# A last product by Strassen's algorithm: seven block products in place of eight, in a single-core gated mix kernel

## The chip, the cores and the metric

The kernel runs on one core of a Trainium2 chip. Its engines work side by side, each through its own queue in program order: TensorE (PE) multiplies matrices into banks of PSUM, VectorE (DVE), ScalarE (ACT) and GpSimd (POOL) work element by element, and SyncE (SP) issues the DMAs. [...] Engines wait for one another through semaphores, and an instruction that waits holds up all that stands behind it on its engine. The metric is the device time in microseconds (us).

## The reference

Input `x` has 2048 tokens of 640 features. A gate `g` for every token mixes two branches:

```python
g = sigmoid((x * gate_w).sum(-1, keepdims=True))
a = conv(x)            # diagonal state-space convolution, kernel K from A, B, C, dt, plus x * Dskip
# linear attention, 32 heads of 20 features
q, k, v = split(x @ wqkv)
phi = lambda t: where(t > 0, t + 1, exp(t)) + 1e-6
kv  = einsum("bhsd,bhse->bhde", phi(k), v);  z = phi(k).sum over tokens
o   = (phi(q) @ kv) / (phi(q) . z + 1e-6)
b   = o @ wo
out = g * a + (1 - g) * b
```

With these inputs the convolution comes down to a running sum of the tokens, scaled by one coefficient for each feature, and `phi(q) @ kv @ wo` to one product of `phi(q)` with a 640 x 640 matrix `M`, in which `kv` and `wo` are already multiplied together.

## The kernel before

The output is made transposed, feature blocks of 128 (five of them, NB) by token groups of 512 (four, NG): 20 output tiles of 128 x 512, numbered j = 5 x group + block. Every product in high accuracy is done three times: both operands are split into a high part (a copy to a shorter format on ACT, `hi`, line 100) and a low part (the difference, on DVE, `lo`, line 103), and `mm3` (lines 106 to 108) adds high x high, low x high and high x low in one bank.

A first stage, up to about 145 us, makes `phi(k)`, its product with `x`, and the convolution tiles y of 16 of the 20 output tiles, which are stored to DRAM. A second, up to about 180 us, builds `M` and begins with q. The part around the change is the third. Its order is written out by hand in `PLAN`, a string of steps that is played from left to right, and the order in which the steps are played is the order of the instructions on every engine:

- `q` (`q_block`): one tile of `phi(q)` before normalisation. 15 matmuls; ACT makes exponential and positive part (lines 648, 649); DVE takes minimum and adds (652) and adds to a weighted sum (658) that becomes the denominator.
- `d` (`q_den`): the denominator of a group. Two matmuls on the high and low part of that sum (673, 674), ACT reads the bank (676), DVE takes the reciprocal (677) and multiplies with 1 - g (680).
- `n` (`q_norm`): scales one tile (688). Its high and low parts, tiles pTh and pTl, are issued by `flush` a step later.
- `f`: `final_mm`, one output tile, 15 matmuls with `M` (5 input blocks x 3), then `final_out`: DVE adds bank and y (727) and SP stores it (728). It then calls `y_block` for a tile that is needed later.
- `y` (`y_block`): loads a stored y (439), or makes it then and there (tiles 16 to 19: ACT 423, DVE scan 424 and multiply-add 427), and POOL multiplies it with the gate (444).

```python
q3 f q3 d2 n2 f q3 n2 f q3 n2 n2 f q3 f n2
f d3 n3 f n3 n3 f n3 f n3 f
f f f f f f
```

These are the last three lines of `PLAN`: five q tiles of group 3 with five outputs between them, group 3's normalisation with five outputs between, and six outputs at the end. PSUM has eight banks here: three with the tag "q", three "f" (outputs and denominators) and two "m". Six buffers hold y tiles, eight (NE) hold tiles of `phi(q)` (tag "e"), and two hold output tiles on their way to DRAM (tag "so").

Of the kernel before, what the change touches and what calls it, by code (L numbers as in the profile page):

```python
# [39 lines left out]
P = 128  # L40
L = 2048
D = 640
NB = D // P
NT = L // P
NG = L // 512
# [12 lines left out]
NK = sum(map(len, CONV_K.values()))  # L58
# [13 lines left out]
NS = NK + PLAN.split().count("c")  # L72


def f32(ap):
    return ap.bitcast(F32)


def body(tc, i, outT):
    nc = tc.nc  # L80
    pe, act, dve, pool, sp = nc.tensor, nc.scalar, nc.vector, nc.gpsimd, nc.sync
    outer, top, kst = ExitStack(), ExitStack(), ExitStack()

    def mk(stack, name, space=None):
        kw = {} if space is None else {"space": space}
        if space is not DRAM:
            kw["reuse_waits"] = "tile"
        return stack.enter_context(tc.tile_pool(name=name, bufs=1, **kw))
# [3 lines left out]
    px = mk(top, "px")  # L92
    pc = mk(top, "pc")
    pw = mk(top, "pw")
# [4 lines left out]
    def hi(dst, src):  # L99
        act.activation(dst, src, AF.Copy)  # L100

    def lo(dst, src, h, eng=None):
        (eng or dve).tensor_tensor(dst, src, f32(h), op=OP.subtract)  # L103

    def mm3(out, ah, al, bh, bl, start, stop):
        pe.matmul(out, ah, bh, start=start, stop=False)  # L106
        pe.matmul(out, al, bh, start=False, stop=False)  # L107
        pe.matmul(out, ah, bl, start=False, stop=stop)  # L108

    def col(tag, n=NB, dt=F32):  # L110
        return pc.tile([P, n], dt, tag=tag, name=tag)
# [20 lines left out]
    zacc = col("zacc", D)  # L132
# [10 lines left out]
    dtc, k0, dsk, lam, ok = [col(n) for n in ("dtc", "k0", "dsk", "lam", "ok")]  # L143
    g, og = col("g", NT), col("og", NT)
# [39 lines left out]
    kp, ke, ks = {}, {}, {}  # L184
# [217 lines left out]
    us, ys, gbs, y_d = {}, {}, {}, {}  # L402

    def gb_load(gi):
        gbs[gi] = pq.tile([P, 512], F32, tag="gb", bufs=NG, name="gb")
        src = g_d[gi * 4 : gi * 4 + 4, :].rearrange("a b -> (a b)")[None, :]
        sp.dma_start(gbs[gi], src.to_broadcast([P, 512]))

    def u_load(j):
        gi, b = divmod(j, NB)  # L410
        if j < NK or j >= NS:
            us[j] = pw.tile([P, D + 2], F32, tag="st", bufs=3, name="u")
        else:
            us[j] = pq.tile([P, 512], F32, tag="u", bufs=1, name="u")
        sp.dma_start(us[j][:, :512], i["xT"][b * P : b * P + P, gi * 512 : gi * 512 + 512])

    def conv(j, name="y"):

        gi, b = divmod(j, NB)
        c = slice(b, b + 1)  # L420
        u = us.pop(j)[:, :512]
        y = pw.tile([P, 512], F32, tag="y", bufs=NY, name=name)
        act.activation(y, u, AF.Copy, scale=k0[:, c])  # L423
        dve.tensor_tensor_scan(y, y, zero.to_broadcast([P, 512]), cY[:, c], op0=OP.add, op1=OP.add)  # L424
        if gi < NG - 1:
            dve.tensor_copy(cY[:, c], y[:, 511:512])
        dve.scalar_tensor_tensor(y, u, dsk[:, c], y, op0=OP.mult, op1=OP.add)
        return y

    def conv_out(j):  # L430
        y = conv(j)
        y_d[j] = dram.tile([P, 512], F32, name=f"y_d{j}")
        sp.dma_start(y_d[j], y)

    def y_block(j):

        if j < NS:
            ys[j] = pw.tile([P, 512], F32, tag="y", bufs=NY, name="yb")
            sp.dma_start(ys[j], y_d[j])
        else:  # L440
            ys[j] = conv(j, "yb")
            if j + 3 < NG * NB:
                u_load(j + 3)
        pool.tensor_tensor(ys[j], ys[j], gbs[j // NB], op=OP.mult)  # L444


# [17 lines left out]
    raw = {}  # L464
# [28 lines left out]
    for b in range(NB):  # L493
        w = raw[b][:, : CA + 2]
# [113 lines left out]
    rem = col("rem", D)  # L608
# [12 lines left out]
    pq = mk(top, "pq")  # L621
    pqp = mk(top, "pqp", PSUM)
# [9 lines left out]
            hi(GT[:, b0:b1, 512:], tp[:, : (b1 - b0) * P].rearrange("p (b s) -> p b s", s=P))  # L632

    pqT, qe, acc, rd = {}, {}, {}, {}
    pend = []

    def q_block(gi, b):

        qp = pqp.tile([P, 512], F32, tag="q", bufs=3, name="qp")
        w, o = (wqA, b * P) if b < 3 else (wqB, (b - 3) * P)  # L640
        for c in range(NB):
            mm3(qp, w[0][:, c, o : o + P], w[1][:, c, o : o + P], xTh[gi][:, c, :], xTl[gi][:, c, :],
                c == 0, c == NB - 1)
        if len(qe) + len(pend) == NE:
# [4 lines left out]
        act.activation(r, qp, AF.Relu)  # L649
        for h, _, v in pend:  # L650
            hi(h, v)
        dve.scalar_tensor_tensor(e, e, 1.0, r, op0=OP.min, op1=OP.add)  # L652
        if b == 0:
            a = acc[gi] = pq.tile([P, 512], F32, tag="acc", bufs=1, name="acc")
            act.activation(a, e, AF.Copy, scale=zc[:, :1])
        else:
            a = acc[gi]
            dve.scalar_tensor_tensor(a, e, zc[:, b : b + 1], a, op0=OP.mult, op1=OP.add)
# [23 lines left out]

    def q_norm(gi, b):
        e = qe.pop((gi, b))
        if b == 0:
            pqT[gi] = [px.tile([P, NB, 512], F32R, tag=f"x{c}{gi}", name=f"pT{c}{gi}") for c in "hl"]
        h, l = [v[:, b, :] for v in pqT[gi]]
        dve.scalar_tensor_tensor(e, e, EPS, rd[gi], op0=OP.add, op1=OP.mult)  # L688
        flush()
        pend.append((h, l, e))  # L690

    def flush():
        for h, l, v in pend:
            hi(h, v)
            lo(l, v, h)
        pend.clear()

    m = {}
# [13 lines left out]
    def final_mm(j):  # L712
        gi, b = divmod(j, NB)
        fps[j] = []
        for h0, h1 in HALVES[j == NG * NB - 1]:
            fp = pqp.tile([P, 512], F32, tag="f", bufs=3, name="fp")
            fps[j].append(fp)
            for kb in range(NB):
                mm3(fp[:, : h1 - h0], m["h"][:, kb, b * P : b * P + P], m["l"][:, kb, b * P : b * P + P],
                    pqT[gi][0][:, kb, h0:h1], pqT[gi][1][:, kb, h0:h1], kb == 0, kb == NB - 1)  # L720

    def final_out(j):
        gi, b = divmod(j, NB)
        o = pq.tile([P, D], F32, tag="so", bufs=2, name="o")
        y = ys.pop(j)
        for fp, (h0, h1) in zip(fps.pop(j), HALVES[j == NG * NB - 1]):
            dve.tensor_tensor(o[:, h0:h1], fp[:, : h1 - h0], y[:, h0:h1], op=OP.add)
            sp.dma_start(outT[b * P : b * P + P, gi * 512 + h0 : gi * 512 + h1], o[:, h0:h1])

    NJ = NG * NB  # L730
    n_q, n_n, n_f, n_y, n_c = 0, 0, 0, 0, NK
    z_part()
    rem_out()
    if NS > NK:
        u_load(NK)
    for w in PLAN.split():
        what, k = w.rstrip("0123456789"), int("0" + w.lstrip("abcdefghijklmnopqrstuvwxyz"))
        if what == "q":
            q_block(*divmod(n_q, NB))
            n_q += 1  # L740
        elif what == "z":
            z_const()
            gates_row()
        elif what == "d":
            q_den(k)
        elif what == "n":
            q_norm(*divmod(n_n, NB))
            n_n += 1
        elif what == "kv":
            kv_mm(k)  # L750
        elif what == "m":
            m_mm(k)
        elif what == "ml":
            m_load()
            for j in range(NS, min(NS + 3, NJ)):
                u_load(j)
        elif what == "c":
            conv_out(n_c)
            n_c += 1
            if n_c < NS:  # L760
                u_load(n_c)
        elif what == "y":
            y_block(n_y)
            n_y += 1
        elif what == "f":
            flush()
            final_mm(n_f)
            final_out(n_f)
            n_f += 1
            if n_y < NJ:  # L770
                y_block(n_y)
                n_y += 1
    assert (n_q, n_n, n_f) == (NJ, NJ, NJ)
# [171 lines left out]
```

## Time and profile before

| | |
|---|---|
| runs | 299.1 us median of 3 (298.33 to 304.32) |
| profiled execution | 296.9 us from the first to the last instruction; no time of its own is given beyond this span |
| busy | PE 98%, weight loads 86%, DVE 77%, ACT 42%, POOL 16% |
| granted PE clock | full throughout |
| DMA | 46.00 MB, mean 155 GB/s |

A row of busy time gives us, share of the span and count of instructions for each engine. In a group of instructions the columns are line, engine, operation, output <- inputs, shape and count, then busy time and mean duration in ns, then idle time of the engine just ahead of them and what ended it. In a row of single instructions the columns are start, duration, engine, line, operation; a number in square brackets is idle time of the engine before it, with what ended it. Weight loads run beside matmuls. The length shown for a matmul is modelled and overlaps with its neighbours; the distance between starts says how long PE takes for one.

### The profile page before, as it was taken

What the parts mean: (1) busy time and instruction counts of PE and PEld (TensorE: products, weight loads), DVE (VectorE), ACT (ScalarE), POOL (GpSimd) and SP (SyncE); (2) the same over time, 40 slices, a digit from 0 to 9 for tenths busy, and PEclk for the clock granted to TensorE, in tenths of its full rate; (3) what the DMA queues carried; (4) which work ended last, traced back from release to release, by engine and by line L of the source; (5) the groups of instructions that cost most, each with busy time, mean ns of one, the idle gap of its engine ahead of it and who ended that gap; (6) DMA issues with size and microseconds to landing.
All of it is one profiled execution on the core that took longest, in us unless ns stands there. A gap on an engine that the chain in (4) does not pass through costs nothing.

```text
span 296.9 us, 4579 instructions
## 1 busy us (share of the span) xinstructions
PE 291.7 (98%) x1627; PEld 254.3 (86%) x1627; DVE 228.6 (77%) x355; ACT 125.1 (42%) x262; POOL 47.0 (16%) x52
## 2 busy tenths in 40 slices
PE   8999999999999999999999999999999999999994
PEld 7998899999999999999887777888888888888884
DVE  2869987899999799955743769968683777787992
ACT  3555144653565545337624374562323233314100
POOL 3601760000000000000000000003313203232541
PEclk9999999999999999999999999999999999999999
DMA  6925477257767854280364563792416022426323
GB/s 171 330 69 184 132 242 232 86 200 234 235 152 256 249 168 156 82 256 1 88 174 138 164 203 106 231 329 79 141 35 186 29 71 71 142 73 182 125 85 111
DMA packets 28409, 46.00 MB, mean 155 GB/s; under 512 B 3771, under 2 KB 10827, under 8 KB 28383
## 3 DMA queue, kind: packets, MB, share of 16 engines
q1 hardware_dynamic: 28383, 45.66, 49.0%
q8 instruction: 15, 0.25, 0.3%
q14 instruction: 11, 0.09, 0.1%
HBM read 32.92 MB, written 12.72 MB: 154 GB/s over the span
## 4 chain that ended last, share of the span: by engine, by line
PE 96%; DMA 1%; SPq 0%; ACT 0%; DVE 0%; issue 0%
PE qp L106 8%; PE fp L107 8%; PE fp L108 8%; PE fp L106 8%; PE qp L107 8%; PE qp L108 8%; PE g L232 6%; PE g L231 6%; PE g L234 6%; PE k L108 6%; PE k L107 6%; PE k L106 6%; PE g L459 3%; PE r L247 2%; PE r L246 2%; PE r L245 2%
## 5 line engine op out<-in xcount | busy, mean ns | idle before, releaser
L444 POOL TENSOR_TENSOR yb<-yb,gb 128x512 f32<-128x512 f32 x20 | 28.3, 1417 | 217.8 <-DMA yb<-y_d 199.6
L108 PE MATMUL fp<-pTl,Mh 128*128 128x512 f32 (+1 forms) x105 | 39.8, 379 | 0.0
L107 PE MATMUL fp<-pTh,Ml 128*128 128x512 f32 (+1 forms) x105 | 39.8, 379 | 0.0
L106 PE MATMUL fp<-pTh,Mh 128*128 128x512 f32 (+1 forms) x105 | 39.8, 379 | 0.0
L232 PE MATMUL g<-ph,xl 128*128 128x512 f32 x80 | 31.4, 392 | 0.0
L231 PE MATMUL g<-ph,xh 128*128 128x512 f32 x80 | 31.3, 391 | 0.0
L652 DVE SCALAR_TENSOR_TENSOR qe<-qe,qr 128x512 f32<-128x512 f32 x20 | 14.3, 716 | 21.7 <-ACT qr L649 21.6
L100 ACT ACTIVATE pTh<-qe 128x512 fp32r<-128x512 f32 x20 | 12.6, 633 | 41.4 <-DVE qe L688 41.4
L210 DVE SCALAR_TENSOR_TENSOR e<-e,r 128x320 f32<-128x320 f32 x32 | 15.7, 496 | 13.2 <-ACT e L207 13.2
L106 PE MATMUL qp<-xTh,wqAh 128*128 128x512 f32 x60 | 23.8, 396 | 0.0
L648 ACT ACTIVATE qe<-qp 128x512 f32<-128x512 f32 x20 | 11.9, 595 | 28.0 <-PE qp L108 23.0
L204 ACT ACTIVATE e<-k 128x320 f32<-128x320 f32 x12 | 5.3, 438 | 43.4 <-PE k L108 43.4
L107 PE MATMUL qp<-xTh,wqAl 128*128 128x512 f32 x60 | 23.4, 390 | 0.0
L108 PE MATMUL qp<-xTl,wqAh 128*128 128x512 f32 x60 | 23.4, 389 | 0.0
L234 PE MATMUL g<-pl,xh 128*128 128x512 f32 x80 | 23.3, 389 | 0.0
L106 PEld LDWEIGHTS fp<-pTh,Mh 128*128 128x128 f32 x105 | 19.8, 188 | 3.8
L107 PEld LDWEIGHTS fp<-pTh,Ml 128*128 128x128 f32 x105 | 19.7, 188 | 3.8
L108 PEld LDWEIGHTS fp<-pTl,Mh 128*128 128x128 f32 x105 | 19.7, 188 | 3.7
L103 DVE TENSOR_TENSOR pTl<-qe,pTh 128x512 fp32r<-128x512 f32 x20 | 16.1, 817 | 6.8 <-ACT pTh L100 6.3
L424 DVE TENSOR_TENSOR_SCAN y<-y,cY,zero 128x512 f32<-128x512 f32 x16 | 20.5, 1278 | 0.8 <-ACT y L423 0.8
L108 PE MATMUL k<-wkBl,xTh 128*128 128x320 f32 x60 | 18.5, 309 | 0.0
L107 PE MATMUL k<-wkBh,xTl 128*128 128x320 f32 x60 | 18.5, 309 | 0.0
(171 smaller groups left out, 720.9 us busy)
## 6 DMA issues: line engine op xcount, KB each, us to landing
xraw<-in_x SPq DMA_DIRECT2D x16, 320.0 KB, 4.4
u<-in_xT SPq DMA_DIRECT2D x20, 256.0 KB, 5.7
out_T<-o SPq DMA_DIRECT2D x19, 256.0 KB, 2.6
y_d<-y SPq DMA_DIRECT2D x16, 256.0 KB, 2.4
yb<-y_d SPq DMA_DIRECT2D x16, 256.0 KB, 3.1
xTraw<-in_xTt SPq DMA_DIRECT2D x12, 320.0 KB, 4.5
Wv<-in_wv SPq DMA_DIRECT2D x5, 320.0 KB, 5.8
Mh<-M_dh SPq DMA_DIRECT2D x5, 320.0 KB, 4.5
```

The source lines that it names most:

```text
L100: act.activation(dst, src, AF.Copy)
L103: (eng or dve).tensor_tensor(dst, src, f32(h), op=OP.subtract)
L106: pe.matmul(out, ah, bh, start=start, stop=False)
L107: pe.matmul(out, al, bh, start=False, stop=False)
L108: pe.matmul(out, ah, bl, start=False, stop=stop)
L210: dve.scalar_tensor_tensor(e, e, 1.0, r[:, :n], op0=OP.min, op1=OP.add)
L231: pe.matmul(gps[b], xh[:, s], h[:, :512], start=t == 0, stop=False)
L232: pe.matmul(gps[b], xl[:, s], h[:, :512], start=False, stop=False)
L234: pe.matmul(gps[b], xh[:, b * P : b * P + P], l[:, :512], start=False, stop=t == NT - 1)
L424: dve.tensor_tensor_scan(y, y, zero.to_broadcast([P, 512]), cY[:, c], op0=OP.add, op1=OP.add)
L444: pool.tensor_tensor(ys[j], ys[j], gbs[j // NB], op=OP.mult)
L652: dve.scalar_tensor_tensor(e, e, 1.0, r, op0=OP.min, op1=OP.add)
```

## The change

The output tiles of token groups 2 and 3 and feature blocks 0 to 3, over input blocks 0 to 3, are taken as a 2 x 2 block product: `M`'s 512 x 512 corner in four blocks, and the normalised `phi(q)` of the two groups in four blocks (input blocks 0 and 1, or 2 and 3; group 2 or 3). Strassen's algorithm in its form with few additions (seven products, chained sums) makes the four results out of seven products of sums. Input block 4 is added with plain matmuls (`rest`), and outputs 14 and 19 (feature block 4) stay whole.

- `t_sums` (step t) makes the sums of `M` on POOL, 4 additions of 512 columns and 8 of 256; `t_split` (step tb) makes their high and low parts in tiles that held weights of q.
- `s_sums` (step s, twice) makes the sums of `phi(q)` in place on POOL, 4 additions each, in the `e` tiles, which `er` keeps for it; `s_split` makes the high and low parts of the four sums.
- `last_pair` runs the products after the plan has ended. Banks are used as running sums: ACT takes a snapshot of a bank in the middle, DVE adds an earlier product onto a bank, and POOL adds a snapshot to the y of another output.
- The plan: outputs 6 to 9 move behind the last q tile, all outputs of groups 2 and 3 move into `last_pair`. `y_block` follows the new order `ORD`, group 3 is normalised in the order 0, 2, 1, 3, 4 (`NORM`), and tiles 16 to 19 load their inputs in the order `LATE`. `e` has 10 buffers in place of 8; two of the four tiles of the gate (`gb`) go to other tiles.

```diff
-NE = 8
+NE = 10
+SG = 2, 3
+ORD = [0, 1, 2, 3, 4, 5, 6, 7, 8, 9, 14, 10, 11, 12, 15, 17, 13, 16, 18, 19]
+NORM = [(g, b) for g in range(NG) for b in ((0, 2, 1, 3, 4) if g == SG[1] else range(NB))]
...
-q3 f q3 d2 n2 f q3 n2 f q3 n2 n2 f q3 f n2
-f d3 n3 f n3 n3 f n3 f n3 f
-f f f f f f
+q3 f q3 d2 n2 q3 n2 t q3 n2 n2 f q3 n2 y
+f d3 tb n3 f n3 s n3 y f n3 s n3 y f
...
+    def t_sums():
+        tr = [pw.tile([P, D + 2], F32, tag=t, bufs=n, name="tr")[:, :512] for t, n in (("wo", 2), ("wo", 2), ("st", 3), ("st", 3))]
+        tt = pool.tensor_tensor
+        for k in range(4):
+            tt(tr[k], f32(m["h"][:, k, :512]), f32(m["l"][:, k, :512]), op=OP.add)
+        for j in range(2):
+            b11, b12, b21, b22 = tr[j][:, :256], tr[j][:, 256:], tr[j + 2][:, :256], tr[j + 2][:, 256:]
+            tt(b11, b12, b11, op=OP.subtract)
+            tt(b12, b22, b12, op=OP.subtract)
+            tt(b22, b22, b11, op=OP.subtract)
+            tt(b21, b21, b22, op=OP.subtract)
+        tw["raw"] = tr
+
+    def t_split():
...
+        for h, r in zip(tw["h"], tr):
+            hi(h, r)
+        for h, l, r in zip(tw["h"], tw["l"], tr):
+            lo(l, r, h)
+
+    def s_sums(j):
+        a11, a12, a21, a22 = er[2, j], er[2, j + 2], er[3, j], er[3, j + 2]
+        tt = pool.tensor_tensor
+        tt(a22, a21, a22, op=OP.add)
+        tt(a21, a11, a21, op=OP.subtract)
+        tt(a11, a22, a11, op=OP.subtract)
+        tt(a12, a12, a11, op=OP.subtract)
+        sx[1, j], sx[3, j], sx[2, j], sx[4, j] = a22, a21, a11, a12
+
+    def s_split(*ks):
...
+        for n, k in enumerate(ks):
+            for j in range(2):
+                sh[k, j] = h[:, 2 * n + j, :], l[:, 2 * n + j, :]
+                hi(sh[k, j][0], sx[k, j])
+            for j in range(2):
+                lo(sh[k, j][1], sx.pop((k, j)), sh[k, j][0])
+
+    PROD = {1: ("x", 0, 0, "m", 0, 0), 2: ("x", 0, 2, "m", 2, 0), 4: ("x", 1, 2, "t", 2, 0),
+            3: ("s", 4, 0, "m", 2, 2), 5: ("s", 1, 0, "t", 0, 0), 6: ("s", 2, 0, "t", 2, 2), 7: ("s", 3, 0, "t", 0, 2)}
...
+        def raws(i):
+            four[i] = pb("m")
+            prod(four[i], 4, i, True)
+            rest(four[i], 1, i)
+            prod(one[i], 2, i, False)
+            rest(one[i], 0, i)
+            done(0, i, one[i])
+
+        def six(i):
+            A[i] = pb(("f", "q")[i])
+            prod(A[i], 6, i, True)
+            dve.tensor_tensor(A[i], A[i], s1[i], op=OP.add)
+            add(0, i + 2, snap(A[i], "r", 2))
+
+        def five(i):
+            B[i] = pb("f")
+            prod(B[i], 5, i, True)
+            add(1, i + 2, snap(B[i], "r", 2))
+
+        def seven(i):
+            prod(A[i], 7, i, False)
+            add(1, i, snap(A[i], "d"))
+            done(1, i, four[i])
+
+        def three(i):
+            prod(B[i], 3, i, False)
+            rest(B[i], 0, i + 2)
+            done(0, i + 2, B[i])
+
+        def end(i):
+            rest(A[i], 1, i + 2)
+            done(1, i + 2, A[i])
+
+        final_mm(last[0])
+        for i in range(2):
+            one[i] = pb("q")
+            prod(one[i], 1, i, True)
+            s1[i] = snap(one[i], ("acc", "accl")[i])
+        final_out(last[0])
+        y_next()
+        s_split(2, 1)
+        raws(0)
+        s_split(3, 4)
+        raws(1)
+        six(0), five(0), six(1), seven(0), three(0), five(1), end(0)
+        seven(1), three(1), end(1)
+        final_mm(last[1])
+        final_out(last[1])
```

In it `prod` issues the six matmuls of one half (128 output columns) of a product, `rest` three, `snap` is a copy of a bank on ACT, `add` an addition to a y tile on POOL, and `done` the addition of bank and y on DVE with the store, followed by the next `y_block`. A step s begins with `flush`.

More of the change, by code (lines that the diff above doesn't have):

```diff
@@ L690, in q_norm @@
         pend.append((h, l, e))
+        if gi in SG and b < 4:
+            er[gi, b] = e
     def flush():
@@ new lines, in prod @@
+    def prod(bank, p, i, first):
+        a, n, k0, w, w0, c = PROD[p]
+        c = slice((c + i) * P, (c + i + 1) * P)
+        for j in range(2):
+            if a == "x":
+                ah, al = [v[:, k0 + j, :] for v in pqT[SG[n]]]
+            else:
+                ah, al = sh[n, j]
+            if w == "m":
+                bh, bl = [m[x][:, w0 + j, c] for x in "hl"]
+            else:
+                bh, bl = [tw[x][w0 + j][:, c] for x in "hl"]
+            mm3(bank, bh, bl, ah, al, first and j == 0, j == 1, skip_group_check=True)
@@ L746, in body @@
         elif what == "n":
-            q_norm(*divmod(n_n, NB))
+            q_norm(*NORM[n_n])
             n_n += 1
+        elif what == "t":
+            t_sums()
+        elif what == "tb":
+            t_split()
+        elif what == "s":
+            flush()
+            s_sums(n_s)
+            n_s += 1
         elif what == "kv":
@@ L754, in body @@
             m_load()
-            for j in range(NS, min(NS + 3, NJ)):
+            for j in LATE[:2]:
                 u_load(j)
```

77 lines of the change are left out of this document (61 added, 16 removed).

## The prediction

> **What bounds the kernel now.** I read the head of the page first, then the waits of TensorE (PE), then busy time by stretch, then the groups of VectorE (DVE) in the part that changes, and last the single instructions of DVE and GpSimd (POOL) there.
>
> ```profile
> span 296.9 us, 4579 instructions
> PE 291.7 (98%) x1627; PEld 254.3 (86%) x1627; DVE 228.6 (77%) x355; ACT 125.1 (42%) x262; POOL 47.0 (16%) x52
> ...
> PE 96%; DMA 1%; SPq 0%; ACT 0%; DVE 0%; issue 0%
> ...
> L100 ACT ACTIVATE pTh<-qe 128x512 fp32r<-128x512 f32 x20 | 12.6, 633 | 41.4 <-DVE qe L688 41.4
> ```
>
> The second row is busy time by engine, the third the chain that ended last: 96% of it is PE. The fourth is a group (count, busy us, mean ns), one copy on ScalarE (ACT), used below. The view of waits, cut to PE, says what PE waited for:
>
> ```profile
> PE k L131 <- POOL ones L122: 1.0, 1, 1.0
> PE r L459 <- ACT wkBh L100: 0.2, 1, 0.2
> ```
>
> That is 1.2 us in all, both at the start. PE's order is fixed by the program and it never stands still later. By stretch:
>
> ```profile
> 220.00:240.00 20.00, 20.00 (x90) 16.53 (x89) 12.84 (x15) 6.61 (x12) 4.36 (x3) 1.00 0.26 80
> ...
> 232.00:293.00 61.00, 60.95 (x283) 50.84 (x281) 50.73 (x57) 14.68 (x25) 18.96 (x13) 1.00 0.30 100
> ```
>
> The columns are the stretch, its length, then PE, weight loads, DVE, ACT, POOL (each with its count), granted clock, DMA share, GB/s. 89 loads in 20 us make 0.225 us for a 512-wide matmul, so a block of 15 takes 3.4 us. In the last 61 us DVE is busy 50.7 us already: PE bounds, and DVE is close behind.
>
> **What the change removes.** The last product takes three matmuls per pair of 128-blocks. The Strassen part (two groups, four output blocks, four input blocks) was 2 x 4 x 4 x 3 = 96 matmuls and becomes 7 products x 2 halves x 2 blocks x 3 = 84. The 24 for the fifth input block and the two whole outputs of the fifth block stay. So 12 matmuls go: 12 x 0.225 = **2.7 us off PE**, 0.9% of the time. A difference under 2%, some 6 us, can hardly be told from no change here, so PE's gain alone cannot show.
>
> **What it adds.** On POOL: `t_sums`, 4 additions of 512 columns and 8 of 256; `s_sums`, 2 x 4 of 512; in `last_pair` 6 additions of 512. On DVE: 4 low parts in `t_split`, 8 in the two `s_split`, 2 additions onto a bank. On ACT: 12 copies for high parts and 8 snapshots of banks, near the 0.63 us of the row L100 each, 13 us on an engine that is busy 14.7 of 61 us; these count only where someone waits. DMAs: same outputs, same loads, another order. The question is what POOL and DVE do to each other. Single instructions (start, duration, engine, line):
>
> ```profile
> 248.67 2.39 DVE L103 TENSOR_TENSOR pTl<-qe,pTh 128x512 fp32r<-128x512 f32 x2
> 279.54 1.99 DVE L424 TENSOR_TENSOR_SCAN yb<-yb,cY,zero 128x512 f32<-128x512 f32 x1
> 259.50 3.35 DVE L677 RECIPROCAL d<-d 128x512 f32<-128x512 f32 x1 [0.18 <-ACT d L676]
> ...
> 248.67 1.84 POOL L444 TENSOR_TENSOR yb<-yb,gb 128x512 f32<-128x512 f32 x1 [2.82 <-DVE qe L688]
> 259.94 1.30 POOL L444 TENSOR_TENSOR yb<-yb,gb 128x512 f32<-128x512 f32 x1 [3.17 <-DMA yb<-y_d]
> 279.16 1.29 POOL L444 TENSOR_TENSOR yb<-yb,gb 128x512 f32<-128x512 f32 x1 [0.69 <-DVE yb L427]
> ```
>
> At 248.67 both start together. POOL's 1.30 becomes 1.84, and the two DVE operations end at 251.06: one DVE operation (0.55), then POOL (1.29), then the other, one after the other. The scan at 279.54 takes 1.99 because POOL holds on until 280.45. The reciprocal, with one operand, delays nobody. So a DVE operation with two SBUF operands and a POOL operation exclude each other for their whole length. With long queues on both sides they take turns:
>
> ```profile
> 36.30 0.90 DVE L217 SCALAR_TENSOR_TENSOR pl<-e,ph 128x640 fp32r<-128x640 f32 x1
> 37.12 1.08 DVE L219 TENSOR_TENSOR zacc<-zacc,e 128x640 f32<-128x640 f32 x1
> ...
> 36.48 1.04 POOL L368 TENSOR_TENSOR cv<-cv,cv 128x128 f32<-128x128 f32 x1
> 37.59 0.93 POOL L369 TENSOR_TENSOR cv<-cv 128x128 f32<-128x128 f32 x1
> ...
> 38.90 0.46 POOL L368 TENSOR_TENSOR cv<-cv,cv 128x128 f32<-128x128 f32 x1
> ```
>
> POOL's 0.46 takes 1.04 behind L217 and 0.93 behind L219; L219 waits for the POOL operation between them. From 0.46 at 128 columns and 1.30 at 512, a 256-wide POOL operation is an estimated 0.74. [...]
>
> [...] The DVE groups from 226 us to the end, with counts:
>
> ```profile
> L103 DVE TENSOR_TENSOR pTl<-qe,pTh 128x512 fp32r<-128x512 f32 x10 | 9.3, 945 | 4.4 <-ACT pTh L100 4.2
> L424 DVE TENSOR_TENSOR_SCAN yb<-yb,cY,zero 128x512 f32<-128x512 f32 x4 | 7.3, 1814 | 0.0
> L688 DVE SCALAR_TENSOR_TENSOR qe<-qe,d 128x512 f32<-128x512 f32 x10 | 7.2, 733 | 0.1
> ...
> L658 DVE SCALAR_TENSOR_TENSOR acc<-qe,zc,acc 128x512 f32<-128x512 f32 x4 | 3.9, 982 | 0.1
> L427 DVE SCALAR_TENSOR_TENSOR yb<-u,dsk,yb 128x512 f32<-128x512 f32 x4 | 3.9, 965 | 0.1
> L652 DVE SCALAR_TENSOR_TENSOR qe<-qe,qr 128x512 f32<-128x512 f32 x4 | 2.8, 690 | 5.8 <-ACT qr L649 5.8
> L680 DVE TENSOR_TENSOR d<-d,og 128x512 f32<-128x512 f32 x2 | 1.4, 692 | 0.2
> ...
> L103 DVE TENSOR_TENSOR accl<-acc,acch 128x512 fp32r<-128x512 f32 x1 | 0.7, 693 | 0.8 <-ACT acch L100 0.8
> ```
>
> 35 of 0.6 us and 4 scans of 1.2 make 25.8 us, and the 13 POOL multiplications of the stretch row 13 x 1.28 = 16.6: 42 us of the 61 that PE still has. The change adds 12 low parts (7.2), 18 POOL additions of 512 (23.0) and 8 of 256 (5.9): **78.5 us**, where PE has 58.3 left. [...]
>
> **The walk.** [...] The rows that it starts from:
>
> ```profile
> 231.88 1.76 POOL L444 TENSOR_TENSOR yb<-yb,gb 128x512 f32<-128x512 f32 x1 [1.59 <-DMA yb<-y_d]
> ...
> 234.11 3.34 DVE L677 RECIPROCAL d<-d 128x512 f32<-128x512 f32 x1
> 237.56 0.69 DVE L680 TENSOR_TENSOR d<-d,og 128x512 f32<-128x512 f32 x1
> 252.69 0.69 DVE L652 SCALAR_TENSOR_TENSOR qe<-qe,qr 128x512 f32<-128x512 f32 x1 [1.02 <-ACT qr L649]
> 254.93 0.69 DVE L103 TENSOR_TENSOR accl<-acc,acch 128x512 fp32r<-128x512 f32 x1 [0.76 <-ACT acch L100]
> 255.53 0.69 DVE L727 TENSOR_TENSOR o<-fp,yb 128x512 f32<-128x512 f32 x1
> ...
> 258.11 0.40 PE L673 MATMUL dp<-acch,bm 128*128 128x512 f32 x1
> ```
>
> 1. `t_sums` stands behind the multiplication of y7 (231.88), so it starts at 233.6. Three additions fit under the reciprocal, the fourth ends at 238.7. Then eight of 0.74 alternate with eight DVE operations of 0.6 to 249.8, where DVE alone would be at 243. Four more for group 2 and the addition of f5 take DVE to 252.9; from min-and-add to the low part of the denominator's sum the rows 252.69 and 254.93 give 2.9, so it is ready at 255.9. PE gets to the denominator product (258.11 before, less three blocks that now stand later) at 247.9: **8.0 us wait**.
> 2. DVE goes on without a gap: the last of group 2 behind the multiplications of y8 and y9, addition f6 at 259.1, reciprocal to 262.5, four low parts of `t_split` behind y14's multiplication, then group 3's first scaling, its high part, its low part, and only then the addition of f7, at 269.4. Output 14 needs f7's bank, PE is there at 266.6: **2.9**.
> 3. The first `s_sums` waits for the load of y10, sent behind f7's store (DVE 255.53 to POOL 259.94: 3.7 us from the end of an addition to POOL). From 273 on it alternates with DVE, so group 3's blocks 3 and 4 are ready at 277.0 and 280.6; the fourth product and its rest get there at 276.2 and 277.7: **3.7**.
> 4. The second `s_sums` stands behind y11 and y12, and beside y17's scan; the low part of its third sum is there at 292.4. PE is before product six at 287.4: **5.0**.
> 5. DVE then has two more low parts between POOL's y15, y17 and y13, an addition, a scan, four low parts, an addition and a scan, all ahead of the addition onto product six's bank at 306.0. Its snapshot is ready at 307.4, and product seven, which writes the same bank, could run at 296.5 without the two waits there: **10.9**. Another 0.4 lies before product three's second half.
> 6. At the end six POOL additions and y19 lie ahead of four additions and the two halves of output 19. The stores have two buffers:
>
> ```profile
> 292.01 0.42 DVE L727 TENSOR_TENSOR o<-fp,yb 128x256 f32<-128x256 f32 x1 [1.86 <-DMA out_T<-o]
> 292.99 0.42 DVE L727 TENSOR_TENSOR o<-fp,yb 128x256 f32<-128x256 f32 x1 [0.56 <-PE fp L108]
> ```
>
> The last addition comes 3.6 us behind PE instead of 0.5 (the row 292.01 shows a wait of 1.9 for a store): **3.1**.
>
> Sum against the profiled execution: 296.9 - 2.7 + 8.0 + 2.9 + 3.7 + 5.0 + 10.9 + 0.4 + 3.1 = 328.2 us of span. The page gives that execution no time beyond its span; the median of the runs, 299.1, is 2.2 above it and the fastest 1.4. So **330 us**, 10% slower.
>
> Costed at nothing: more `e` buffers and `gb` in other tiles (same loads); the moved f6 to f9 and output 14, whose 17 us of PE should cover the new sums and do so in part, which is why the waits aren't longer. If an unqueued 256-wide addition took 0.46 us, as the 128-wide one, the bill falls by 2.2; at 1.30 it rises by 4.5.
>
> **The rivals.** *Side by side*: DVE and POOL with long queues don't block each other as the short meetings did, DVE passes first or POOL fits into gaps. It decides at 238 to 250 us: if DVE's operations there stay at 0.69, the low part of the denominator's sum is ready near 248.7, the wait is 0.8, output 14 waits about 0.8, and the end is 296.9 - 2.7 + 1.6 + 2.2 = 298: no change. For it speaks that DVE, with 50.7 us and 14 operations of 0.69 more, 60 in all for PE's 58, would all but fit; against it every meeting in the rows. *Half-blocking*: some of the turns are cheaper, or DVE wins them; the waits of PE halve, to 15, and the tail to 1.5: 296.9 - 2.7 + 15 + 1.5 + 2.2 = 313. Against it stands the bill, which no order shortens. *The cold clock*: PE would stand still five times for over 2 us, which the trace before never shows (clock 1.00, longest wait 1.0). The rows give PE's waits no price beyond their length; if the clock fell to half for some 3 us after each of the three long ones, it would cost 1.5 us each, mostly hidden where DVE is the later one: 333. [...] *Not what it says*: PE would show 315 matmuls on the final product still; the loops count 303.
>
> **How the numbers follow.** Forecast 330 us (318 to 338): 0.67. Cold clock, 333: 0.10. Half-blocking, 305 to 317: 0.10. Side by side, 296 to 303: 0.12. Faster by over 2% would need more than PE's whole gain: 0.01. The range runs from 312, inside half-blocking, to 340, the upper bound of the 256-wide addition. Slower: 0.67 + 0.10 + 0.10 = 0.87; same 0.12; faster 0.01.
>
> **What would show it.** The waits view lists PE waiting for DVE's `accl`, for an addition (bank of f7), for low parts and for snapshots, together some 30 us; POOL's busy time near doubles from 47 us; DVE's mean for low parts rises above 1.2 us in the last part; 303 matmuls on the final product. It is wrong if PE stays without waits, or if DVE's operations beside `t_sums` keep 0.69.

## The result and the profile after

| | before | after |
|---|---|---|
| median of the runs | 299.25 us (4 runs) | 330.75 us (4 runs, 330.41 to 331.25) |
| ratio | 1 | 1.107, interval 1.105 to 1.109 |
| profiled execution, span | 296.9 us | 328.8 us |
| matmuls | 1627 | 1615 |

The change makes the kernel 31.5 us slower. One of the four runs before, 304.32 us, is a slow one, and the ratio leaves it out. The twelve matmuls are gone, as counted. The head of the page of the kernel after, with busy time by engine (us, share of the span, instructions) and the granted clock in 40 slices:

```profile
span 328.8 us, 4612 instructions
...
PE 298.1 (91%) x1615; PEld 256.4 (78%) x1615; DVE 247.1 (75%) x369; ACT 135.7 (41%) x282; POOL 82.9 (25%) x78
...
PEclk9999999999999999999999999999998799797696
```

PE, which bounded the kernel before with 98%, is at 91%; POOL went from 47.0 to 82.9 us. The clock, full throughout before, now drops in six slices, all in the last quarter; the last of them lies behind PE's last matmul. The view of waits, cut to PE (us in total, times, longest), shows what took PE's place:

```profile
PE fs L109 <- ACT snap L826: 11.1, 2, 9.8
PE dp L680 <- ACT acch L103: 5.6, 1, 5.6
PE fs L111 <- DVE sl L106: 2.0, 3, 0.7
PE fs L109 <- ACT pTh L103: 1.5, 1, 1.5
...
PE fp L109 <- DVE o L736: 0.5, 1, 0.5
```

(Lines have moved: the split is now at 103 and 106, the matmul triple at 109 to 111, the snapshots of banks at 826, POOL's late additions at 831, the addition of a snapshot to product six's bank at 852, the output additions at 736 and 742. Min-and-add is 659, the weighted sum 665, the scaling 695, the first step of y tiles 16 to 19 is 429, the sums of the matrix are 754 to 760. The experiments' edits move some lines by a few more.) The longest two are the denominator product of group 3 and product seven. Single instructions of PE at these two places (start, length shown, line; in brackets the wait):

```profile
253.71 0.79 PE L680 MATMUL dp<-acch,bm 128*128 128x512 f32 x1 [5.63 <-ACT acch L103]
254.43 0.79 PE L681 MATMUL dp<-accl,bm 128*128 128x512 f32 x1
255.02 0.63 PE L109 MATMUL fp<-pTh,Mh 128*128 128x512 f32 x1
255.45 0.63 PE L110 MATMUL fp<-pTh,Ml 128*128 128x512 f32 x1
...
305.75 0.80 PE L109 MATMUL fs<-sh,tAh 128*128 128x512 f32 x1 [9.75 <-ACT snap L826]
306.34 0.63 PE L110 MATMUL fs<-sh,tAl 128*128 128x512 f32 x1
```

Behind each of the two waits the matmuls start 0.43 us apart instead of 0.225. There are 23 such distances in three stretches of about 4, 2 and 4 us, and they add 23 x 0.2 = 4.6 us to PE. In busy time by stretch (length, PE, weight loads, DVE, ACT, POOL, clock, DMA share, GB/s) the same is seen as a clock of 0.50:

```profile
296.00:302.00 6.00, 0.00 (x0) 0.00 (x0) 5.56 (x7) 1.86 (x4) 1.64 (x1) 0.82 0.17 58
302.00:308.00 6.00, 2.25 (x5) 1.83 (x6) 3.25 (x4) 2.03 (x4) 3.46 (x3) 0.50 0.12 44
```

From 296 to 302 PE does nothing, and DVE is busy 5.56 of 6 us: the rest waits for DVE's queue. What that queue does before product seven may run:

```profile
289.46 4.59 DVE L106 TENSOR_TENSOR sl<-qe,sh 128x512 fp32r<-128x512 f32 x3 [4.56 <-ACT sh L103]
...
297.44 3.56 DVE L106 TENSOR_TENSOR sl<-qe,sh 128x512 fp32r<-128x512 f32 x4
...
304.37 1.29 DVE L852 TENSOR_TENSOR fs<-fs,snap 128x512 f32<-128x512 f32 x2
310.81 0.69 DVE L742 TENSOR_TENSOR o<-fs,yb 128x512 f32<-128x512 f32 x1 [5.14 <-POOL yb L831]
...
321.87 0.69 DVE L742 TENSOR_TENSOR o<-fs,yb 128x512 f32<-128x512 f32 x1 [2.26 <-DMA out_T<-o]
323.59 0.76 DVE L736 TENSOR_TENSOR o<-fp,yb 128x256 f32<-128x256 f32 x2 [1.03 <-PEq L971]
```

It stands idle 4.56 us for the high part of POOL's second set of sums, then has low parts, two scans and two output additions in program order, and only at 304.37 makes the addition that product seven's bank waits for. The last two rows are the end: PE's last matmul starts at 320.90, the last additions run until 324.35.

That DVE and POOL take turns is seen in both queues beside the sums of the matrix. DVE first, then POOL:

```profile
239.22 1.11 DVE L695 SCALAR_TENSOR_TENSOR qe<-qe,d 128x512 f32<-128x512 f32 x1
240.25 1.23 DVE L659 SCALAR_TENSOR_TENSOR qe<-qe,qr 128x512 f32<-128x512 f32 x1
```

```profile
238.60 1.18 POOL L757 TENSOR_TENSOR tr<-tr 128x256 f32<-128x256 f32 x1
239.86 1.07 POOL L758 TENSOR_TENSOR tr<-tr 128x256 f32<-128x256 f32 x1
```

Each queue moves one instruction in about 1.15 us. (Four of 512 columns stand ahead of them on POOL, from 232.7 us on.)

### The profile page after: what moved, and what is told of

The parts are those of the page before. It is cut to its first block, busy times and chain, and to the rows that moved or that the text cites. A ratio compares the mean times of both kernels' runs of the same rounds, so it can differ in the third digit from the quotient of the medians.

```text
span 328.8 us, 4612 instructions
## 1 busy us (share of the span) xinstructions
PE 298.1 (91%) x1615; PEld 256.4 (78%) x1615; DVE 247.1 (75%) x369; ACT 135.7 (41%) x282; POOL 82.9 (25%) x78
## 5 line engine op out<-in xcount | busy, mean ns | idle before, releaser
L450 POOL TENSOR_TENSOR yb<-yb,gb 128x512 f32<-128x512 f32 x20 | 30.7, 1546 | 208.1 <-DMA yb<-y_d 177.8
L659 DVE SCALAR_TENSOR_TENSOR qe<-qe,qr 128x512 f32<-128x512 f32 x20 | 15.7, 784 | 18.8 <-ACT qr L656 18.8
L109 PE MATMUL fp<-pTh,Mh 128*128 128x512 f32 (+1 forms) x65 | 25.1, 386 | 0.5 <-DVE o L736 0.5
L111 PE MATMUL fp<-pTl,Mh 128*128 128x512 f32 (+1 forms) x65 | 25.0, 384 | 0.0
L110 PE MATMUL fp<-pTh,Ml 128*128 128x512 f32 (+1 forms) x65 | 25.0, 384 | 0.0
L109 PE MATMUL qp<-xTh,wqAh 128*128 128x512 f32 x60 | 23.8, 396 | 0.0
L109 PE MATMUL k<-wkAh,xTh 128*128 128x322 f32 x60 | 18.5, 309 | 0.0
L111 PE MATMUL k<-wkAl,xTh 128*128 128x322 f32 x60 | 18.5, 308 | 0.0
L110 PE MATMUL k<-wkAh,xTl 128*128 128x322 f32 x60 | 18.5, 308 | 0.0
```

The source lines that it names most:

```text
L109: pe.matmul(out, ah, bh, start=start, stop=False, **kw)
L110: pe.matmul(out, al, bh, start=False, stop=False, **kw)
L111: pe.matmul(out, ah, bl, start=False, stop=stop, **kw)
```

## The experiments

Times are set against 330.75 us for the changed kernel and 299.0 to 299.3 us for the kernel before in the same comparisons. Where a time stands without an interval it is a single run; the repeated kernels here spread by 1 to 3 us.

**Which part costs what.** The first four take parts away or move them.

The order alone: plan, order of the y tiles and buffers of the changed kernel, ten plain outputs at the end.

```diff
-        final_mm(last[0])
...
-        s_split(2, 1)
-        raws(0)
...
-        final_out(last[1])
+        for j in (14, 10, 11, 15, 12, 17, 16, 13, 18, 19):
+            final_mm(j)
+            final_out(j)
+            y_next()
...
-            t_sums()
+            pass
...
-            t_split()
+            pass
...
-            s_sums(n_s)
+            pass
```

> The changed order alone: plan, y order and buffers of the changed kernel, but the ten outputs of groups 2 and 3 as plain products (150 matmuls in place of 138) and no sums and splits of Strassen's algorithm. Theory (POOL's sums and DVE exclude each other): the denominator product of group 3 waits about 1 us, output 14 about 1 us, the rest nothing: 299 to 302 us. Rival (the order: the denominator one block behind its q, outputs behind the banks of late additions): the wait of 5.6 us before the denominator product stays, and the time is 306 us or more.

Measured: **305.04 us**, ratio 1.019 (1.017 to 1.022). Both theories missed. In PE's waits the denominator product takes 0.8 us, so the rival's mechanism is not there, but four outputs wait for a bank:

```profile
PE fp L109 <- DVE o L736: 3.8, 4, 1.7
...
PE dp L680 <- ACT acch L103: 0.8, 1, 0.8
```

The additions that free these banks stand behind group 3's scalings in DVE's queue, and between scaling and low part DVE itself waits for the copy on ACT:

```profile
268.11 0.68 DVE L695 SCALAR_TENSOR_TENSOR qe<-qe,d 128x512 f32<-128x512 f32 x1
269.48 0.69 DVE L106 TENSOR_TENSOR pTl<-qe,pTh 128x512 fp32r<-128x512 f32 x1 [0.70 <-ACT pTh L103]
270.09 0.68 DVE L736 TENSOR_TENSOR o<-fp,yb 128x512 f32<-128x512 f32 x1
```

So 5.8 us come with the order (and the buffers that changed with it, which this run does not separate), with no Strassen in it: more than twice what the twelve matmuls can give.

All 26 additions on POOL left out:

```diff
-        for k in range(4):
-            tt(tr[k], f32(m["h"][:, k, :512]), f32(m["l"][:, k, :512]), op=OP.add)
...
-            tt(b21, b21, b22, op=OP.subtract)
+        tr = [f32(m["h"][:, k, :512]) for k in range(4)]
...
-        tt(a22, a21, a22, op=OP.add)
-        tt(a21, a11, a21, op=OP.subtract)
-        tt(a11, a22, a11, op=OP.subtract)
-        tt(a12, a12, a11, op=OP.subtract)
...
-            pool.tensor_tensor(y, y, v, op=OP.add)
```

> All 26 added POOL additions left out (the sums of M, the sums of q, the additions of snapshots to y), so the output is not the reference's; the splits on ACT and DVE, the seven products, the snapshots and the order stay. Theory: 299 to 304 us; before product seven some 2 us of wait are left, from the scans and low parts that stand ahead on DVE. Rival (DVE's own queue and the chain of banks, without POOL): over 312 us, product seven still waits 8 us or more.

Measured: **315.48 us**. The additions are worth 15.3 us, about half; the theory, that they are nearly all, falls. The rival's time holds, its wait of 8 us not quite: without any of the additions product seven still waits 6.8 us:

```profile
PE fs L109 <- ACT snap L813: 8.1, 2, 6.8
```

Only the twelve sums of the matrix left out (the first part of the edit above):

> Only the 12 POOL additions of the sums of M left out (their splits read M's high part, so the output is not the reference's). Theory: the wait of 5.6 us before the denominator product falls to 1.5 us or less, DVE's operations at 238 to 250 us return to 0.69 us, and the time falls by 4 to 7 us, to 324 to 327 us; the wait of 10 us before product seven stays. Rival (that wait comes from the order): it stays over 4 us, and the time is 329 us or more.

Measured: **326.67 us**, 4.1 less, as the theory had it. The denominator's wait falls from 5.6 to 0.8 us, output 14 waits 2.6 instead of 0.5, and product seven's wait stays at 9.7.

The same 26 additions on DVE, nothing left out:

```diff
-        tt = pool.tensor_tensor
+        tt = dve.tensor_tensor
...
-            pool.tensor_tensor(y, y, v, op=OP.add)
+            dve.tensor_tensor(y, y, v, op=OP.add)
```

> All 26 added additions on DVE instead of POOL, at the same places of the program. [...] Rival (DVE's queue alone is the bound and POOL relieves it): slower than 335 us.

Measured: **331.85 us**: no gain, and not the rival's 335 either. There is no turn-taking beside the sums any more, and they are cheaper one by one:

```profile
241.51 0.69 DVE L695 SCALAR_TENSOR_TENSOR qe<-qe,d 128x512 f32<-128x512 f32 x1
242.12 2.49 DVE L754 TENSOR_TENSOR tr<-Mh,Ml 128x512 f32<-128x512 f32 x4
244.53 0.42 DVE L757 TENSOR_TENSOR tr<-tr 128x256 f32<-128x256 f32 x1
```

But they stand in DVE's queue ahead of what PE waits for, and PE waits 6.6 us at the denominator, 8.3 for group 3's blocks and 5.0 before product seven. Held up by POOL or by its own additions, DVE delivers equally late.

**Turns or delay.** To tell what POOL's reads do to DVE from the mere time that POOL takes, the additions were replaced by memsets of about the same length, which read nothing; none of the 26 sums is made, the late additions are replaced like those of `s_sums`. The 16 memsets for the matrix take 9.8 us, where the additions alone would take some 11.0 (4 x 1.28 + 8 x 0.74); three for a 512-wide addition take 1.43 us for its 1.28:

```diff
-            tt(tr[k], f32(m["h"][:, k, :512]), f32(m["l"][:, k, :512]), op=OP.add)
...
+        for k in (0, 0, 1, 1, 2, 2, 3, 3, 0, 2, 0, 2, 1, 3, 1, 3):
+            pool.memset(trs[k], 1.0)
...
-        tt(a22, a21, a22, op=OP.add)
...
+        for v in (a22, a21, a11, a12):
+            pool.memset(v, 1.0)
+            pool.memset(v, 1.0)
+            pool.memset(v[:, :256], 1.0)
```

> POOL's 26 added additions replaced by fills of the same tiles that take as long (642 columns for some 0.64 us, 512 and 512 and 256 for some 1.3) but read nothing, so the output is not the reference's. POOL's queue and the waits for what it writes stay; the reading at the same time as DVE goes. Theory (POOL's reading holds up DVE's operations with two SBUF operands, and this makes the 15 us between 330.75 and the 315.5 without POOL's sums): DVE's operations at 238 to 250 us take 0.69 us, the wait before the denominator product is 1 us, the time 316 to 322 us. Rival (the length of POOL's queue and those who wait for its results): 327 us or more.

Measured: **325.6 us**, between the two. DVE's rows beside the memsets, its first wait for POOL's second set, and its wait for the late ones:

```profile
239.72 0.69 DVE L659 SCALAR_TENSOR_TENSOR qe<-qe,qr 128x512 f32<-128x512 f32 x1
240.44 0.75 DVE L665 SCALAR_TENSOR_TENSOR acc<-qe,zc,acc 128x512 f32<-128x512 f32 x1
...
283.98 2.98 DVE L106 TENSOR_TENSOR sl<-qe,sh 128x512 fp32r<-128x512 f32 x3 [6.10 <-ACT sh L103]
...
305.21 0.69 DVE L742 TENSOR_TENSOR o<-fs,yb 128x512 f32<-128x512 f32 x1 [5.84 <-POOL yb L827]
```

```profile
233.62 9.76 POOL L753 MEMSET tr<- 128x642 f32 x16
```

POOL is busy without a gap from 233.6 to 243.4 and DVE runs at its own 0.69 and 0.75 (1.23 and 1.11 beside the additions). So it is POOL's reading that blocks DVE, and that is worth 5.1 of the 15.3 us (each of the two times is a single run). The other 10.1 stay: the waits of 6.10 and 5.84 us are for POOL's results, and PE's wait before product seven is 9.9 us as before.

**The order of DVE's queue before product seven.** The scans of y16 and y18 moved behind product six's addition (`done` with a last argument of False doesn't call `y_next`), with POOL's additions and without:

```diff
-            done(0, i, one[i])
+            done(0, i, one[i], False)
...
-        six(0), five(0), six(1), seven(0), three(0), five(1), end(0)
+        six(0), five(0), six(1), y_next(), y_next(), seven(0), three(0), five(1), end(0)
```

> The changed kernel with one thing moved: the y tiles 16 and 18 (copy, scan, multiply-add, POOL's multiplication) are made behind product six, not ahead of it. Theory (DVE's order ahead of the addition onto product six's bank): the wait before product seven falls from 9.9 to 3 to 6 us and the time by 3 to 6 us, to 325 to 328 us. Rival (the snapshot is late for the low parts and POOL): the wait stays over 8 us, and the time is 329 us or more.

Measured: **331.06 us**, ratio 1.107 (1.100 to 1.114). Product seven's wait fell to 3.4 us as said, and the time did not move: it is the rival's. A new wait stands before product three's second half:

```profile
PE fs L109 <- ACT snap L826: 9.2, 3, 4.4
```

```profile
301.05 1.32 ACT L429 ACTIVATE yb<-u,k 128x512 f32<-128x512 f32 x2
...
311.03 0.72 ACT L429 ACTIVATE yb<-u,k 128x512 f32<-128x512 f32 x1 [8.17 <-DVE o L742]
311.66 0.58 ACT L826 ACTIVATE snap<-fs 128x512 f32<-128x512 f32 x1
```

The snapshot at 311.66, which product three needs, stands in ACT's queue behind the first step of y19, and that waits 8.17 us for an output addition on DVE. That addition in turn needs POOL's late ones.

> The kernel without POOL's added additions (output not the reference's) and with the y tiles 16 and 18 behind product six. Theory: product seven's wait falls from 6.8 to under 2 us, and the time from 315.5 to 306 to 311 us, near the 305 of the order alone. Rival (what is left over the order's cost comes from the splits and the chain of banks, not from the scans): 313 us or more.

Measured: **313.22 us**, just in the rival's range. That is 2.3 less than with the scans in their place, which two single runs hardly show; here too product seven no longer waits, and product three waits 2.1 us instead.

**The clock.** 24 and 42 matmuls that nobody reads, ahead of the two long waits, keep PE busy:

```diff
+        if gi == 3:
+            for _ in range(24):
+                pe.matmul(dp, bm, m["h"][:, 0, :512], start=True, stop=True)
...
-        six(0), five(0), six(1), seven(0), three(0), five(1), end(0)
+        six(0), five(0), six(1)
+        dummy = pb("q")
+        for _ in range(42):
+            pe.matmul(dummy, bm, m["h"][:, 0, :512], start=True, stop=True)
+        seven(0), three(0), five(1), end(0)
```

> The changed kernel with 24 matmuls without use ahead of the denominator product of group 3 and 42 ahead of product seven, which fill PE's two longest waits (5.6 and 9.8 us), so that the granted clock stays full behind them. Theory (DVE is late behind each of these waits anyway): the matmuls behind both waits return from 0.43 to 0.227 us, and the time moves by less than 1 us. Rival (the lower clock costs): 2 to 4 us less, 327 to 329 us.

Measured: **328.25 us**, ratio 1.098 (1.095 to 1.102), mean clock 0.987 instead of 0.961:

```profile
PEclk9999999999999999999999999999999999799996
```

So 2.5 us of the loss are the clock; two of its three slow stretches are gone, the one at 281 us stays. It is more than the "less than 1" of the theory and less than PE's 4.6 us, since behind the first stretch output 14's wait grew from 0.5 to 2.7 us.

**Low parts and banks.** The twelve low parts of the sums, with and without POOL's additions:

```diff
-        for h, l, r in zip(tw["h"], tw["l"], tr):
-            lo(l, r, h)
+        tw["l"] = tw["h"]
...
-            for j in range(2):
-                lo(sh[k, j][1], sx.pop((k, j)), sh[k, j][0])
```

> Leaves out all 26 additions on POOL and also the 12 low parts of the splits on VectorE (the second of each three matmuls reads the high part again). Products, banks, snapshots and order stay those of the change. The kernel without POOL's additions alone took 315.5 us, the one with the order alone 305.0. Theory (the low parts, 12 x 0.69 = 8.3 us in VectorE's queue ahead of the additions that the banks wait for, make that gap): the wait of product seven falls from 7.0 us to under 2, time 303 to 308. Rival (the round trips by way of the banks make it: product, addition on the bank, snapshot, next product on the same bank, and the clock behind them): seven still waits over 4 us, time 311 or more.

Measured: **308.86 us**, ratio 1.031 (1.028 to 1.034), just above the theory's range, with its wait under 2 us:

```profile
PE fs L109 <- ACT snap L810: 3.0, 2, 1.6
```

The low parts are 6.6 of the 10.4 us that lie between the order alone and the kernel without additions. The other 3.8 are left with the block products, their snapshots and the high parts on ACT; they hold PE's gain of 2.7 already. In the two profiled executions, 4.2 us apart, PE's last matmul starts only 0.6 us later than with the order alone (300.03 for 299.43): 5.5 us of gaps from 268 us on and 1.6 us of half clock stand against the 2.7 and against the 4.0 us of gaps that the order alone has from 264 us on. The rest lies behind PE. The last additions wait for the store of an earlier one, and the end comes 5.1 us after them instead of 3.4:

```profile
301.96 0.76 DVE L736 TENSOR_TENSOR o<-fp,yb 128x256 f32<-128x256 f32 x2 [3.22 <-DMA out_T<-o]
```

> Leaves out only the 12 low parts of the splits on VectorE; POOL's 26 additions stay. Changed kernel 330.75 us. Theory (each low part takes its own 0.69 us and mostly a turn with POOL, so 12 of them are 8 to 14 us of the chain that ends last): 317 to 323 us, product seven waits 3 to 6 us. Rival (VectorE waits for POOL's results there anyway, the low parts fill time that is lost): 326 us or more.

Measured: **321.75 us**, ratio 1.077 (1.075 to 1.079), in the theory's range; product seven waits 5.8 us. With POOL's additions beside them the low parts are worth 9.0 us.

**Repairs.** The sums of the matrix one group earlier, then the same with two more repairs:

```diff
-q2 q2 y q2 d1 n1 f q2 n1 y f q2 n1 n1 f n1 f
-q3 f q3 d2 n2 q3 n2 t q3 n2 n2 f q3 n2 y
+q2 t q2 y q2 d1 n1 f q2 n1 y f q2 n1 n1 f n1 f
+q3 f q3 d2 n2 q3 n2 q3 n2 n2 f q3 n2 y
```

> The sums of the matrix (t) are made one group earlier, behind the first projection block of group 2, with nothing left out. Without these sums the kernel took 326.7 us, with them in their place 330.75. Theory (where they stand now they cost 4 us by exclusion and by the wait of group 3's denominator; earlier, TensorE has blocks in store and the same turns cost nobody): 326 to 328, denominator product of group 3 waits about 1 us. Rival (the turns move along and delay group 1's or group 2's normalisation): 329.5 or more, with a new wait of TensorE before 220 us.

Measured: **326.32 us**, ratio 1.092 (1.090 to 1.094), the theory's. The sums cost the same turns earlier, but PE does not wait there; the denominator of group 3 waits 1.4 us. Where DVE pauses, a 256-wide addition shows its own length:

```profile
208.22 1.19 POOL L757 TENSOR_TENSOR tr<-tr 128x256 f32<-128x256 f32 x1
209.49 0.74 POOL L758 TENSOR_TENSOR tr<-tr 128x256 f32<-128x256 f32 x1
```

> Three repairs together, nothing left out: t one group earlier, the two scans moved behind product six's addition, the six late additions on VectorE in place of POOL. Theory (each repair takes away a wait that the others don't bring back; the late additions, 6 x 0.69 = 4 us, go through VectorE without the way over POOL's queue): 317 to 323. Rival (VectorE is the bound from 270 us on, so what it is given is what the end moves by): 325 to 330. Neither has it below the kernel before, 299.

Measured: **323.69 us**, ratio 1.082 (1.079 to 1.086), just above the theory's range: the repairs add up in part. Two waits of 3.5 and 3.7 us for snapshots remain. No version here comes near 299 us, and with every added sum and low part left out the kernel is still at 308.9.

The loss in steps, each the difference of two kernels above:

| step | us |
|---|---|
| order of outputs and y tiles, with its buffers | 305.0 - 299.25 = 5.8 |
| block products, high parts on ACT, snapshots, banks and last stores, with 12 matmuls less | 308.9 - 305.0 = 3.8 |
| twelve low parts on DVE | 315.5 - 308.9 = 6.6 |
| 26 additions on POOL: their reads | 330.75 - 325.6 = 5.1 |
| the same: their time in POOL's queue | 325.6 - 315.5 = 10.1 |

The sizes depend on the sequence, as the 6.6 and 9.0 us of the low parts show; 2.5 us of the clock are contained in them.

## Why the prediction was right, and where its steps were not

The forecast was 330 us and the time is 330.75. The place and kind of the waits came as walked through, but their sizes were 7 us too long in sum, and costs that the sum left out, the half clock above all, made up for it. That the sum of 328.2 us comes so near the span of 328.8 is luck in part.

| step of the walk | said, us | gap in PE, us |
|---|---|---|
| 1 denominator of group 3 | 8.0 | 5.8 |
| 2 output 14 | 2.9 | 0.7 |
| 3 fourth product and its rest | 3.7 | 3.7 |
| 4 product six | 5.0 | 2.0 |
| 5 product seven, with the two waits at product five ahead of it | 10.9 | 11.7 |
| before product three | 0.4 | 0 |
| waits in sum | 30.9 | 23.8 |
| half clock, 23 matmuls | 0 | 4.6 |
| tail behind PE | 3.1 | 2.7 |

(The gaps are distances between starts less 0.227 us. The tail is the end of the last addition less that of the last matmul, 324.35 - 321.2, less the 0.5 of before. These make 296.9 - 2.7 + 23.8 + 4.6 + 2.7 = 325.3. Of the 3.5 us to the span, 1.6 are the first matmuls behind the waits, 0.59 to 0.72 us apart in the rows above, and 1 is the end: 4.45 us from the last addition to the last instruction instead of 3.5. The rest is short pauses.)

- **PE's gain**, 2.7 us for 12 matmuls: 1615 are left, as counted. It is never seen by itself, since PE no longer bounds.
- **Step 1** named the right queue and had one term too large. An addition of 256 columns is 0.74 us, as estimated, but a turn of it with a DVE operation is 1.15 us, not 0.74 + 0.6 = 1.34. Eight turns make 1.5 of the missing 2.2 us. So the two do not exclude each other for quite their whole length, as the prediction had it.
- **Step 2** was mis-sized for two reasons. DVE came earlier by what step 1 had too much, and PE came later because of the half clock behind the denominator. With PE kept busy, output 14's wait is 2.7 us, nearly the 2.9.
- **Step 3** has the right sum, partly for another reason. Of its three gaps, 1.61, 0.45 and 1.61 us, the first two are block 4 of group 3. The third is for the snapshot of product one, which ACT makes only behind the first step of a y tile, which waits for DVE. What the prediction says of ACT's copies, "these count only where someone waits", was true, but the walk did not look who waits: this gap is left even with all sums and low parts out.
- **Step 4** was too long by 3.0 us: POOL's sums took their bare 1.3 us where DVE stood idle waiting for them (the second set ends at 290.1), and the low part that product six needs was there at 290.7, not at 292.4. PE came at 287.5, as said, but the five matmuls of product six that do not need this low part ran ahead of it, which the walk did not count.
- **Step 5** was nearly right, 11.7 for 10.9, and by its mechanism: low parts, additions and two scans ahead of the addition on product six's bank. Taking the low parts out brings product seven's own wait from 9.8 to 5.8 us, moving the scans to 3.4. But the end hardly moves with the scans, since POOL's late additions, y19 and the snapshots end at the same time. A wait of PE was priced as if it were the end; behind it stood DVE, POOL and ACT, nearly as late.
- **The cold clock** was a rival at 333 us, with its cost "mostly hidden". It happened: half rate behind both long waits (5.6 and 9.8 us) and once behind a cluster of short ones (1.45, 0.28 and 1.34 us). Of the five waits of over 2 us that the prediction expects, two came. Filling these two gave back 2.5 us at the end. In the sum the half clock should have been a term. No run had shown the rival's term, half rate for some 3 us behind each of three long waits at 1.5 us each (granted clock before: 1.00); what the kernel after shows in its place is 23 matmuls at 0.43 us in three stretches, 4.6 us. Without the matrix sums the clock was at half behind a wait of 2.6 us too.
- **The bill** of 78.5 us, where PE had 58.3 left, carried the confidence against half-blocking. It does not hold as a floor, since turns are shorter than the sum of their parts (1.15 for 1.34 us), and it is not what sets the end: moving all 26 additions off POOL changed nothing (331.85), and leaving POOL's time but not its reads gave back 5.1 us. What the runs show instead is queues in order, each waiting for the other's results.
- **The moved outputs** were "costed at nothing". Alone, with the y order and the buffers that go with them, they cost 5.8 us: PE waits for output additions behind group 3's scalings on DVE.
- **Side by side** fell by its own test: the operations at 238 to 250 us went to 1.1 to 1.23 us, not 0.69. **Half-blocking** fell in its time; turns are cheaper than full, 1.15 for 1.34, but not by half.
- What should show: PE's waits of "some 30 us" are 22 in the view; POOL is at 82.9; the low parts of the sums have a mean of 1214 ns:

```profile
L106 DVE TENSOR_TENSOR sl<-qe,sh 128x512 fp32r<-128x512 f32 x8 | 9.3, 1214 | 4.6 <-ACT sh L103 4.6
L106 DVE TENSOR_TENSOR pTl<-qe,pTh 128x512 fp32r<-128x512 f32 x10 | 9.1, 919 | 4.3 <-ACT pTh L103 4.2
...
L659 DVE SCALAR_TENSOR_TENSOR qe<-qe,qr 128x512 f32<-128x512 f32 x4 | 4.7, 1164 | 3.8 <-ACT qr L656 3.8
```

The means of normalisation's own low parts did not rise (919 ns, 945 before): only what runs beside POOL's long queues pays.

What stays open: no run splits the 3.8 us of the block products into banks, snapshots and stores; the profiles show that most of it lies behind PE's last matmul. Nor is the order's 5.8 us split between the plan and the buffers.

## What to carry to other kernels

An algorithm that saves an eighth of the matmuls of a block product is paid for in element-wise work, and where the next engine is as busy in that stage as DVE was here (50.7 of 61 us), the saving has to be set against every instruction it adds there, in queue order. Moving work to a free engine hides it only if nobody waits for its results: two thirds of what POOL's additions cost here were the time of POOL's queue and the waits for its results, not contention. Where one wait is taken out, look for what is nearly as late; here three engines were, and of the parts tried only what had slack in front of it (the matrix sums, one group earlier) could be won back whole.

## What the runs showed of the hardware

- A POOL operation that only writes (memset, 16 in 9.76 us) left DVE's operations with two SBUF operands at 0.69 and 0.75 us; one that reads two operands made them 1.1 to 1.23.
- In long turns a 256-wide POOL addition and a 512-wide DVE operation took 1.15 us together (kernel after, 238.6 to 247.8 us), less than the 0.74 and 0.6 that they take alone. On DVE itself the 256-wide addition starts every 0.45 us (sums on DVE, from 244.53 us on).
- Matmuls ran at half rate, 0.43 us between them, behind waits of 5.6 and 9.8 us (kernel after, 3.8 us each), behind 1.45, 0.28 and 1.34 us that followed closely (kernel after, 2.3 us), and behind a wait of 2.6 us (without the matrix sums, 2.6 us). Single instructions of PE without the matrix sums:

```profile
263.17 0.80 PE L109 MATMUL fp<-pTh,Mh 128*128 128x512 f32 x1 [2.61 <-DVE o L736]
263.76 0.63 PE L110 MATMUL fp<-pTh,Ml 128*128 128x512 f32 x1
```

Behind a wait of 3.7 us in the kernel with three repairs it set in only 1 us after PE had started again:

```profile
305.05 0.50 PE L109 MATMUL fs<-sh,Mh 128*128 128x512 f32 x1 [3.69 <-ACT snap L826]
...
306.08 0.62 PE L110 MATMUL fs<-sh,Ml 128*128 128x512 f32 x1
```

The length of a wait alone does not decide. A single wait of 2.4 us brought half rate without POOL's additions, and waits of 1.37 and 0.23 us brought it with the matrix sums one group earlier (0.43 us between matmuls from 251.2 to 254.2 us); waits of 2.4 us (three repairs), 2.7 us (matmuls without use) and 2.8 us (without additions, scans later) did not. All changes of the granted clock that show in one run ahead of PE's last matmul lie whole multiples of 3.41 us apart, to 0.1 us, in every run here that has more than one: in the kernel after it is at half from 252.10 to 258.93, from 279.41 to 282.82 and from 299.89 to 310.13 us, lengths of 6.8, 3.4 and 10.2 us; without the matrix sums the distances of the matmuls change at 266.34, 276.60, 280.01 and 307.34 us. Which waits bring the half rate, the runs do not show.
